# First layers of the paired blocks: three of seven products added in PSUM, attention visits ahead of the fifth product

## The chip, the core and the metric

The kernel runs on one core of one Trainium2 chip. The metric is the device time of one execution in microseconds. Three runs of the kernel before took 792.59, 793.10 and 793.72 us; the median is 793.1 us.

## What is computed

Chunked softmax attention (8 batches, 8 heads, 576 positions of 64 features, in chunks of 64), whose output, laid out as 4608 tokens of 512 features, goes through a two-layer network with a PReLU between:

```python
scores = scale * np.matmul(q_c, k_c.transpose(0, 1, 2, 4, 3))
scores = scores - np.max(scores, axis=-1, keepdims=True)
attn = np.exp(scores)
attn = attn / (np.sum(attn, axis=-1, keepdims=True) + 1e-09)
x = np.matmul(attn, v_c)                  # as tokens: 4608 x 512
h = x @ w_in                              # 512 x 2048
g = np.maximum(h, 0.0) + alpha * np.minimum(h, 0.0)
out = g @ w_out                           # 2048 x 512
```

All of it is float32. A product of two float32 matrices is made of three matmuls on a high and a low part of each operand (high x high, high x low, low x high).

## The kernel before

Tokens come in 36 subtiles of 128 and nine blocks of 512. Attention runs by subtile. A *visit* (`visit`) does the attention of one subtile in two halves: the values (probabilities times v, L361) of the subtile before last, and the scores (L246) of a new one, 32 small matmuls each, into one PSUM tile `ps_a`. Behind them VectorE takes the maximum (L256), ScalarE scales it (L261) and takes eight exponentials, one a head (L263), VectorE normalises (L265 to L267) and transposes (L304), and SP stores and loads the transposed probabilities as `pT` with eight DMAs (L311), for the values of two visits later. ScalarE also copies the values out of `ps_a` into the block's tile xh or xl (L372).

The first three blocks go through both layers plainly, until about 311 us (second layer at L430, its output copied from PSUM at L464). The last six blocks go in three *pairs*. For a pair each layer is a product of 2x2 block matrices made with seven products instead of eight. The first layer of a pair is eight runs of `first_product`, one for each j, of seven products of six matmuls 128x512 (L698), 42 in all. The seven products are summed in four ways; each sum goes through the PReLU into one quarter of g. `prelu` is a negative part on ScalarE (L379) and a multiply-add on VectorE (L382). Four PSUM banks (`ps_o`, called a, c, d and e in `first_product`) take the products; the sums are made in two ways: some products are added to a bank in PSUM, others by VectorE (L720, L727, L728, L738) from a copy that ScalarE makes in SBUF (L719, L726).

The second layer (`second_product`, L841) has 56 steps of six matmuls. Its operands are split into high and low part by a cast on ScalarE (L657) and a subtraction on VectorE (L658), some after an operand subtraction on VectorE (L759); the first few are split while the first layer still runs.

In pairs 0 and 1 each of the eight runs has one visit ahead of it (in the last two of pair 1 with values only); pair 2 has none. Each engine works through its instructions in the order in which the program leaves them. That order comes from a scheduler: instructions under `tc.high_priority` are put forward, and `tc.issue_after` keeps a piece of work behind a named instruction. The visit's softmax is emitted under high priority; TensorE's order is that in which the code is written. Weights of the seven products come from DRAM in units of two products, in the order of the table `ORDERS["wi"]`, through a ring of four buffers that POOL's queue fills (L639).

Of the kernel before, what the change touches and what calls it, by code (L numbers as in the profile page):

```python
# [60 lines left out]
def tile_local_attention_prelu_ffn(  # L61
# [192 lines left out]
    def attn_max(sc3):  # L254
        mx = small.tile([P, H, 1], F32, name="mx", bufs=2)
        return mx, nc.vector.tensor_reduce(mx.rearrange("p (b g) k -> p b (g k)", b=2), sc3, axis=AX.X, op=ALU.max)  # L256

    def attn_softmax(s, sc3, mx, scaled):
        pr = soft.tile([P, H, C], F32, name="pr")
        sm = small.tile([P, H, 1], F32, name="sm", bufs=2)  # L260
        nc.scalar.mul(mx, mx, -SCALE)  # L261
        for g in range(H):
            last = nc.scalar.activation(pr[:, g], sc3[:, g // NP, g % NP], AF.Exp, bias=mx[:, g], scale=SCALE, accum_out=sm[:, g])  # L263
        stages["softmax"] = scaled, last
        nc.vector.tensor_scalar(sm, sm, 1e-9, None, op0=ALU.add)  # L265
        nc.vector.reciprocal(sm, sm)
        nc.vector.tensor_tensor(pr, pr, sm.broadcast_to([P, H, C]), op=ALU.mult)  # L267
        probs[s] = pr

    def early_softmax(s, sc3):  # L270

# [28 lines left out]
    def attn_blocks(s):  # L300

        pr = probs.pop(s)
        tb = stage.tile([P, 2, H, HALF], F32, name="t3", bufs=2)
        nc.vector.transpose(tb.rearrange("p j h t -> p h j t"), pr)  # L304
        pT = load.tile([P, 2, H, HALF], F32, name="pT", bufs=2)
        for c in range(2):
            for i in range(2):
                for j in range(2):
                    src = slice(c * C + i * HALF, c * C + (i + 1) * HALF)
                    dst = slice(c * C + j * HALF, c * C + (j + 1) * HALF)  # L310
                    nc.sync.dma_start(  # L311
                        out=pT[dst, i].rearrange("p h t -> p (h t)"),
                        in_=tb[src, j].rearrange("p h t -> p (h t)"),
                    )
        pdiag[s] = pT
# [68 lines left out]
    def prelu(g, h, f):  # L384
        negative(g, h)
        rectify(g, h, f)
# [95 lines left out]
    phases = [(0, 0, n0), (1, 0, n1), (0, n0, NF), (1, n1, NF)] + [(b, 0, NF) for b in range(2, PLAIN)]  # L482
    x = {0: new_x(), 1: new_x()}

    def visit(old, new):

        ps = ps_a.tile([P, 2, TB], F32, name="ps_a")
        with tc.high_priority(offset=HIGH):
            if old is not None:
                xo = attn_values(old, ps)  # L490
            if new is not None:
                sc3 = attn_scores(new, ps)
                if new + 2 < NSUB:
                    attn_load(new + 2, "q")
                attn_load(new, "v")
            if new is not None:
                attn_softmax(new, sc3, *attn_max(sc3))
            if old is not None:
                attn_x(old, xo)
            if new is not None:  # L500
                attn_blocks(new)

    def visit_two(new):

        tiles = [pool.tile([P, 2, TB], F32, name=name) for pool, name in ((ps_a, "ps_a"), (ps_p, "ps_b"))]
        olds, news = ([s for s in range(n, n + 2) if s < NSUB] for n in (new - 2, new))
        with tc.high_priority(offset=HIGH):
            xs = [attn_values(s, ps) for s, ps in zip(olds, tiles)]
            scores = [attn_scores(s, ps) for s, ps in zip(news, tiles)]
            for s, xo in zip(olds, xs):  # L510
                attn_x(s, xo)
            most = [attn_max(sc3) for sc3 in scores]
        for s in news:
            if s + 2 < NSUB:
                attn_load(s + 2, "q")
            attn_load(s, "v")

        def rest(s, sc3, at):
            attn_softmax(s, sc3, *at)
            attn_blocks(s)  # L520

        return [functools.partial(rest, *args) for args in zip(news, scores, most)]

    def first(which, s, n, queue):

# [38 lines left out]

    ORDERS = {"wi": (5, 7, 1, 6, 3, 4, 2), "wo": (1, 5, 6, 3, 7, 2, 4)}
    units = {side: [dram.tile([P, 2, 2, 2 * P], F32, name=f"{side}_a{n}") for n in range(7 * JF // 2)] for side in ORDERS}

    def unit(side, i, j):  # L570
# [117 lines left out]
    def bank(n):  # L688
        return ps_p.tile([P, TB], F32, name=f"ps_o{n}")
# [10 lines left out]
                    start=first and at == 0, stop=at == n - 1, skip_group_check=not first,  # L700
                ))

    def softmax_behind(read, scored):
        if scored:
            with tc.issue_after(read.ins):
                scored.pop(0)()

    def first_product(ops, g, j, scored):

        def part(ps, i, first):  # L710
            product(ps, weight("wi", i, j), [ops[i, k] for k in range(2)], first)

        c, d, a, e = (bank(n) for n in banks)
        banks[:] = banks[3:] + banks[:3]
        part(c, 5, True)
        part(d, 7, True)
        with tc.high_priority(offset=HIGH):
            t = gp.tile([P, TB], F32, name="gh")
            read = nc.scalar.copy(t, c)  # L719
            nc.vector.tensor_tensor(t, d, t, op=ALU.add)  # L720
        softmax_behind(read, scored)
        part(a, 1, True)
        part(e, 6, True)
        with tc.high_priority(offset=HIGH):
            u = gp.tile([P, TB], F32, name="g")
            read = nc.scalar.copy(u, a)  # L726
            nc.vector.tensor_tensor(u, e, u, op=ALU.add)  # L727
            nc.vector.tensor_tensor(t, t, u, op=ALU.add)  # L728
        softmax_behind(read, scored)
        for n, f in enumerate((j, JF + j)):  # L730
            g[f] = const.tile([P, 2, TB], F32, name=rooms[14 + 2 * j + n])
        with tc.high_priority(offset=HIGH):
            prelu(g[JF + j][:, 1], t, JF + j)
        for ps, i, f, col in ((c, 3, j, 1), (d, 4, JF + j, 0)):
            part(ps, i, False)
            with tc.high_priority(offset=HIGH):
                h = gp.tile([P, TB], F32, name="gl")
                nc.vector.tensor_tensor(h, ps, u, op=ALU.add)  # L738
                prelu(g[f][:, col], h, f)
        part(a, 2, False)  # L740
        with tc.high_priority(offset=HIGH):
            prelu(g[j][:, 0], a, j)

    AHEAD = 2
    EARLIER = 4
# [256 lines left out]
    for pair in range(NPAIR):  # L1002
        b = PLAIN + 2 * pair
        more = pair + 1 < NPAIR
        if more:
            new_raw(b + 2)
        g, scored = {}, []
        for j in range(JF):
            if more:
                visit(new - 2, new if new < NSUB else None)  # L1010
                new += 1
            if j == JF - 1:
                operands = [operand(g, at) for at in range(AHEAD + 1)]
            first_product(ops, g, j, scored)
        if more:
            ops, conversion = convert(b + 2)
        second_product(g, b, operands, conversion, not more)
# [39 lines left out]
```

## Time and profile before

| | |
|---|---|
| median of three runs | 793.1 us (792.59 to 793.72) |
| span of the profiled execution | 791.9 us |
| outside the span, median less span | 1.2 us |
| TensorE busy | 781.9 us (99%) |
| VectorE busy | 654.4 us (83%) |
| ScalarE busy | 448.8 us (57%) |
| first layers of pairs 0, 1, 2 | 85.8, 84.75, 76.1 us |

The span goes from the first to the last instruction that the profiler recorded, and the durations of the rows below are of that one execution. PE is TensorE's matmuls, PEld its weight loads, DVE is VectorE, ACT ScalarE, POOL GpSimd, SP SyncE. In the chain of waits each stretch is put down to the engine on which the end hung. In the timeline a figure in brackets is the idle time ahead of an instruction, and what ended it.

### The profile page before, as it was taken

What the parts mean: (1) busy time and instruction counts of PE and PEld (TensorE: products, weight loads), DVE (VectorE), ACT (ScalarE), POOL (GpSimd) and SP (SyncE); (2) the same over time, 40 slices, a digit from 0 to 9 for tenths busy, and PEclk for the clock granted to TensorE, in tenths of its full rate; (3) what the DMA queues carried; (4) which work ended last, traced back from release to release, by engine and by line L of the source; (5) the groups of instructions that cost most, each with busy time, mean ns of one, the idle gap of its engine ahead of it and who ended that gap; (6) DMA issues with size and microseconds to landing.
All of it is one profiled execution on the core that took longest, in us unless ns stands there. A gap on an engine that the chain in (4) does not pass through costs nothing.

```text
span 791.9 us, 15470 instructions
## 1 busy us (share of the span) xinstructions
PE 781.9 (99%) x5565; PEld 643.2 (81%) x5565; DVE 654.4 (83%) x1153; ACT 448.8 (57%) x1218; POOL 180.9 (23%) x296
## 2 busy tenths in 40 slices
PE   7999999999999999999999999999999999999998
PEld 7788888888888888888888888888888888888886
DVE  6999989997989976877799987777889956679675
ACT  6975555655666565556656546664575444354542
POOL 0053322442324320111111121111211121112110
PEclk9999999999999999999999999999999999999999
DMA  9759495566969675888865778776556766565574
GB/s 345 322 213 363 168 322 197 193 228 184 275 189 285 217 280 172 285 264 272 267 209 196 228 243 281 259 238 193 199 186 220 255 216 190 197 197 188 190 237 158
DMA packets 69467, 184.53 MB, mean 233 GB/s; under 512 B 11008, under 2 KB 18448, under 8 KB 69264
## 3 DMA queue, kind: packets, MB, share of 16 engines
q0 software_dynamic: 34336, 119.56, 45.8%
q1 hardware_dynamic: 34768, 63.60, 23.6%
q8 instruction: 44, 0.72, 0.4%
q10 hardware_dynamic: 288, 0.39, 0.2%
q14 instruction: 31, 0.25, 0.1%
HBM read 135.27 MB, written 42.99 MB: 225 GB/s over the span
## 4 chain that ended last, share of the span: by engine, by line
PE 81%; DVE 6%; ACT 5%; DMA 5%; issue 1%; SPq 1%; POOL 0%; DVEq 0%; ACTq 0%
PE ps_o L698 29%; PE ps_o L841 20%; PE ps_h L394 9%; PE ps_b L841 8%; PE ps_oa L430 5%; PE ps_ob L430 5%; PE ps_a L361 2%; ACT pr L263 1%; DMA pT<-t 1%; PE ps_a L246 1%; DMA wi_a<-raw 1%; DMA raw<-w_out 1%; SPq L311 1%; DMA raw<-w_in 1%; DVE gl L411 1%
## 5 line engine op out<-in xcount | busy, mean ns | idle before, releaser
L394 PE MATMUL ps_h<-xh,wi 128*128 128x512 f32 x384 | 104.5, 394 | 0.2 <-ACT xh L346 0.2
L698 PE MATMUL ps_o<-wi,raw 128*128 128x512 f32 x252 | 99.2, 394 | 0.1
L698 PE MATMUL ps_o<-wo,raw 128*128 128x512 f32 x252 | 98.2, 390 | 0.0
L394 PEld LDWEIGHTS ps_h<-xh,wi 128*128 128x128 f32 x384 | 71.1, 188 | 15.2 <-ACT xh L346 0.4
L263 ACT ACTIVATE pr<-ps_a,mx 128x64 f32<-128x64 f32 x224 | 67.5, 328 | 1.0
L657 ACT CAST gh<-wi 128x512 fp32r<-128x512 f32 x57 | 35.6, 624 | 48.7 <-PE ps_o L841 25.3
L430 PE MATMUL ps_oa<-wo,gh 128*128 128x512 f32 x192 | 59.9, 393 | 0.0
L430 PE MATMUL ps_ob<-wo,gh 128*128 128x512 f32 x192 | 59.1, 389 | 0.0
L698 PEld LDWEIGHTS ps_o<-wi,raw 128*128 128x128 f32 x252 | 47.3, 188 | 10.3 <-ACT wi L464 0.2
L698 PEld LDWEIGHTS ps_o<-wo,raw 128*128 128x128 f32 x252 | 47.3, 188 | 9.6
L394 PE MATMUL ps_h<-xl,wi 128*128 128x512 f32 x192 | 52.0, 390 | 0.0
L698 PE MATMUL ps_o<-wi,wi 128*128 128x512 f32 x126 | 49.6, 394 | 0.0
L698 PE MATMUL ps_o<-wi,wo 128*128 128x512 f32 x126 | 49.6, 394 | 0.0
L263 ACT ACTIVATION_READ_ACCUMULATOR pr<-ps_a,mx 128x1 f32 x224 | 49.3, 220 | 0.0
L698 PE MATMUL ps_o<-wo,wo 128*128 128x512 f32 x126 | 49.1, 390 | 0.0
L698 PE MATMUL ps_o<-wo,wi 128*128 128x512 f32 x126 | 49.1, 390 | 0.0
L408 ACT CAST gh<-g 128x512 fp32r<-128x512 f32 x48 | 30.2, 630 | 31.8 <-DVE g L382 25.8
L720 DVE TENSOR_TENSOR gh<-ps_o,gh 128x512 f32<-128x512 f32 x24 | 16.6, 691 | 38.1 <-ACT gh L719 20.5
L658 DVE TENSOR_TENSOR gl<-wi,gh 128x512 fp32r<-128x512 f32 x54 | 37.2, 690 | 13.1 <-ACT gh L657 12.8
L379 ACT ACTIVATE wo<-gh 128x512 f32<-128x512 f32 x24 | 15.2, 633 | 53.5 <-DVE gh L728 53.5
L639 POOL DMA_DIRECT2D raw<-wi_a x42 | 22.3, 531 | 100.8 <-PE ps_o L698 86.5
L639 POOL DMA_DIRECT2D raw<-wo_a x42 | 22.2, 529 | 94.2 <-PE ps_o L841 52.3
(296 smaller groups left out, 2108.9 us busy)
## 6 DMA issues: line engine op xcount, KB each, us to landing
raw<-wi_a POOLq DMA_DIRECT2D x42, 512.0 KB, 4.5
raw<-wo_a POOLq DMA_DIRECT2D x42, 512.0 KB, 4.4
wi<-wi_a POOLq DMA_DIRECT2D x21, 512.0 KB, 4.5
wo<-wi_a POOLq DMA_DIRECT2D x21, 512.0 KB, 4.7
wi<-wo_a POOLq DMA_DIRECT2D x21, 512.0 KB, 4.3
wo<-wo_a POOLq DMA_DIRECT2D x21, 512.0 KB, 4.5
k_sb<-kT SPq DMA_DIRECT2D x28, 256.0 KB, 4.9
q_sb<-qT SPq DMA_DIRECT2D x28, 256.0 KB, 4.9
```

Of the source, the lines that this page charges most:

```text
L263: last = nc.scalar.activation(pr[:, g], sc3[:, g // NP, g % NP], AF.Exp, bias=mx[:, g], scale=SCALE, accum_out=sm[:, g])
L361: pe(nc.tensor.matmul(ps[par * C:(par + 1) * C, c, hp * C:(hp + 1) * C], lhsT=v_sb[rows, h * C:(h + 1) * C], rhs=p[rows, :, par * NP + hp] ...
L379: nc.scalar.activation(g, h, AF.Relu, scale=-1.0)
L394: pe(nc.tensor.matmul(hps, lhsT=wi[f][:, l, k * P:(k + 1) * P], rhs=xx[:, k], start=(i == 0 and k == 0), stop=(i == 2 and k == NK - 1),))
L408: nc.scalar.copy(gh, g)
L430: pe(nc.tensor.matmul(o, lhsT=a[:, ts], rhs=wo[f][:, l], start=(f == first and i == 0), stop=(f == last and i == 2),))
L639: streamed[0] = nc.gpsimd.dma_start(out=f32(t), in_=units[side][n])
L657: hi = nc.scalar.copy(t_hi, t)
L658: return hi, nc.vector.tensor_tensor(t_lo, t, f32(t_hi), op=ALU.subtract)
L698: pe(nc.tensor.matmul(ps, lhsT=w[:, l, k * P:(k + 1) * P], rhs=xx[:, xl], start=first and at == 0, stop=at == n - 1, skip_group_check=not ...
L720: nc.vector.tensor_tensor(t, d, t, op=ALU.add)
L841: pe(nc.tensor.matmul(ps[m], lhsT=w[:, l, m * P:(m + 1) * P], rhs=xx, start=begins and j == 0 and n == 0, stop=j == JF - 1 and n == 2, ski ...
```

## The change

The order of the seven products in a run goes from 5, 7, 1, 6, 3, 4, 2 to 1, 7, 6, 2, 5, 4, 3. Product 1 goes into bank a. ScalarE copies bank a into bank e, from PSUM to PSUM, and product 6 is added there by TensorE. The sum is copied in the same way into bank c, to which products 5 and then 3 are added; product 2 is added to bank a, product 4 to bank e. Product 7 is copied from bank d into SBUF (v), and VectorE adds it twice: to bank c after product 5 (t) and to bank e after product 4 (u). So a run has two VectorE additions in place of five and three ScalarE copies in place of two, two of them into PSUM; the 42 matmuls stay. The visit of a run now stands after product 2, ahead of the fifth product, in place of ahead of the run. In a visit of a pair the copy of the values now stands ahead of the maximum, and the normalisation, the transpose and its DMAs come behind u. The banks no longer change their parts from run to run.

```diff
@@ -262,10 +262,14 @@
         for g in range(H):
             last = nc.scalar.activation(pr[:, g], sc3[:, g // NP, g % NP], AF.Exp, bias=mx[:, g], scale=SCALE, accum_out=sm[:, g])
         stages["softmax"] = scaled, last
+        return s, pr, sm
+
+    def attn_normalize(s, pr, sm):
         nc.vector.tensor_scalar(sm, sm, 1e-9, None, op0=ALU.add)
         nc.vector.reciprocal(sm, sm)
         nc.vector.tensor_tensor(pr, pr, sm.broadcast_to([P, H, C]), op=ALU.mult)
         probs[s] = pr
+        attn_blocks(s)
 
...
-    def visit(old, new):
+    def visit(old, new, in_pair=False):
 
         ps = ps_a.tile([P, 2, TB], F32, name="ps_a")
         with tc.high_priority(offset=HIGH):
@@ -493,33 +497,16 @@
                 if new + 2 < NSUB:
                     attn_load(new + 2, "q")
                 attn_load(new, "v")
-            if new is not None:
-                attn_softmax(new, sc3, *attn_max(sc3))
-            if old is not None:
+            if in_pair:
                 attn_x(old, xo)
             if new is not None:
-                attn_blocks(new)
...
+                parts = attn_softmax(new, sc3, *attn_max(sc3))
+                if in_pair:
+                    return functools.partial(attn_normalize, *parts)
+            if old is not None and not in_pair:
+                attn_x(old, xo)
+            if new is not None:
+                attn_normalize(*parts)
...
-    ORDERS = {"wi": (5, 7, 1, 6, 3, 4, 2), "wo": (1, 5, 6, 3, 7, 2, 4)}
+    ORDERS = {"wi": (1, 7, 6, 2, 5, 4, 3), "wo": (1, 5, 6, 3, 7, 2, 4)}
...
-    def softmax_behind(read, scored):
-        if scored:
-            with tc.issue_after(read.ins):
-                scored.pop(0)()
-
-    def first_product(ops, g, j, scored):
+    def first_product(ops, g, j, between):
 
         def part(ps, i, first):
             product(ps, weight("wi", i, j), [ops[i, k] for k in range(2)], first)
 
-        c, d, a, e = (bank(n) for n in banks)
-        banks[:] = banks[3:] + banks[:3]
-        part(c, 5, True)
+        a, d, e, c = (bank(n) for n in banks)
+        for n, f in enumerate((j, JF + j)):
+            g[f] = const.tile([P, 2, TB], F32, name=rooms[14 + 2 * j + n])
+        part(a, 1, True)
+        with tc.high_priority(offset=HIGH):
+            nc.scalar.copy(e, a)
         part(d, 7, True)
         with tc.high_priority(offset=HIGH):
-            t = gp.tile([P, TB], F32, name="gh")
-            read = nc.scalar.copy(t, c)
-            nc.vector.tensor_tensor(t, d, t, op=ALU.add)
-        softmax_behind(read, scored)
-        part(a, 1, True)
-        part(e, 6, True)
+            v = gp.tile([P, TB], F32, name="g")
+            nc.scalar.copy(v, d)
+        part(e, 6, False)
         with tc.high_priority(offset=HIGH):
-            u = gp.tile([P, TB], F32, name="g")
-            read = nc.scalar.copy(u, a)
-            nc.vector.tensor_tensor(u, e, u, op=ALU.add)
-            nc.vector.tensor_tensor(t, t, u, op=ALU.add)
-        softmax_behind(read, scored)
-        for n, f in enumerate((j, JF + j)):
-            g[f] = const.tile([P, 2, TB], F32, name=rooms[14 + 2 * j + n])
-        with tc.high_priority(offset=HIGH):
-            prelu(g[JF + j][:, 1], t, JF + j)
-        for ps, i, f, col in ((c, 3, j, 1), (d, 4, JF + j, 0)):
-            part(ps, i, False)
-            with tc.high_priority(offset=HIGH):
-                h = gp.tile([P, TB], F32, name="gl")
-                nc.vector.tensor_tensor(h, ps, u, op=ALU.add)
-                prelu(g[f][:, col], h, f)
+            nc.scalar.copy(c, e)
         part(a, 2, False)
         with tc.high_priority(offset=HIGH):
             prelu(g[j][:, 0], a, j)
+        normalize = between()
+        part(c, 5, False)
+        with tc.high_priority(offset=HIGH):
+            t = gp.tile([P, TB], F32, name="gh")
+            nc.vector.tensor_tensor(t, c, v, op=ALU.add)
+            prelu(g[JF + j][:, 1], t, JF + j)
+        part(e, 4, False)
+        with tc.high_priority(offset=HIGH):
+            u = gp.tile([P, TB], F32, name="gl")
+            summed = nc.vector.tensor_tensor(u, e, v, op=ALU.add)
+            if normalize:
+                with tc.issue_after(summed.ins):
+                    normalize()
+            prelu(g[JF + j][:, 0], u, JF + j)
+        part(c, 3, False)
+        with tc.high_priority(offset=HIGH):
+            prelu(g[j][:, 1], c, j)
 
...
-        g, scored = {}, []
+        g = {}
         for j in range(JF):
+            between = lambda: None
             if more:
-                visit(new - 2, new if new < NSUB else None)
+                between = functools.partial(visit, new - 2, new if new < NSUB else None, True)
                 new += 1
             if j == JF - 1:
                 operands = [operand(g, at) for at in range(AHEAD + 1)]
-            first_product(ops, g, j, scored)
+            first_product(ops, g, j, between)
         if more:
             ops, conversion = convert(b + 2)
         second_product(g, b, operands, conversion, not more)
```

Three places show how the engines' orders change. The first is TensorE, at the end of the plain phase (`ps_ob` is its last output bank) and the start of pair 0. Here before:

```order
L430 MATMUL ps_ob<-wo_1527,gl 128x512
L361 MATMUL ps_a<-pT,v_sb 64x64 x16
L246 MATMUL ps_a<-k_sb,q_sb 64x64 x16
L698 MATMUL ps_o_4038<-wi_3807,raw 128x512
L698 MATMUL ps_o_4038<-wo_3808,raw 128x512
```

And now, where `ps_o_3971` is bank a, `ps_o_3972` d, `ps_o_3973` e and `ps_o_3974` c:

```order
L434 MATMUL ps_ob<-wo_1527,gl 128x512
L685 MATMUL ps_o_3971<-wi_3434,raw 128x512
L685 MATMUL ps_o_3971<-wo_3435,raw 128x512
...
L685 MATMUL ps_o_3972<-wi_3798,raw 128x512
...
L685 MATMUL ps_o_3973<-wi_3847,raw 128x512
...
L685 MATMUL ps_o_3971<-wi_3589,raw 128x512
...
L365 MATMUL ps_a<-pT,v_sb 64x64 x16
L246 MATMUL ps_a<-k_sb,q_sb 64x64 x16
L685 MATMUL ps_o_3974<-wi_3807,wi_3924 128x512
```

The first visit has moved from between the two phases to behind four products of the first run.

The second is VectorE in the first run of pair 0, from the end of the plain phase's work. Before (`mx` is the maximum, `gh`, `g` and `gl` the sums, `ta` and `tb` the high and low part of a split operand):

```order
L256 TENSOR_REDUCE mx<-ps_a 128x8
L720 TENSOR_TENSOR gh<-ps_o_4039,gh 128x512
L265 TENSOR_SCALAR sm<-sm 128x8
L266 RECIPROCAL sm<-sm 128x8
L267 TENSOR_TENSOR pr<-pr,sm 128x512
L304 STREAM_TRANSPOSE t_4027<-pr 128x8x2x32
L727 TENSOR_TENSOR g<-ps_o_4041,g 128x512
L728 TENSOR_TENSOR gh<-gh,g 128x512
L738 TENSOR_TENSOR gl<-ps_o_4038,g 128x512
```

And now (L715 is t, L720 is u):

```order
L386 SCALAR_TENSOR_TENSOR wi_3975<-wi_3975,rise,ps_o_3971 128x512
L645 TENSOR_TENSOR tb<-wi_3975,ta 128x512
L256 TENSOR_REDUCE mx<-ps_a 128x8
L715 TENSOR_TENSOR gh<-ps_o_3974,g 128x512
L720 TENSOR_TENSOR gl<-ps_o_3973,g 128x512
L386 SCALAR_TENSOR_TENSOR wo_3976<-wo_3976,rise,gh 128x512
L268 TENSOR_SCALAR sm<-sm 128x8
L269 RECIPROCAL sm<-sm 128x8
L270 TENSOR_TENSOR pr<-pr,sm 128x512
L386 SCALAR_TENSOR_TENSOR wo_3976<-wo_3976,rise,gl 128x512
L386 SCALAR_TENSOR_TENSOR wi_3975<-wi_3975,rise,ps_o_3974 128x512
L308 STREAM_TRANSPOSE t_4085<-pr 128x8x2x32
```

Three additions are gone; product 2's prelu and the split of its result now stand ahead of the maximum, and the maximum stands directly ahead of t. On ScalarE the cast for that split (L644) stands between the negative part of product 2 and the copy of the values, and the maximum waits for the copy. The second run has a split (into `more`) at the same place.

The third is VectorE in the sixth run of pair 0 and the visit in it. Before, between the prelu that ends the fifth run and the run's first addition:

```order
L382 SCALAR_TENSOR_TENSOR wi_4781<-wi_4781,rise,ps_o_4744 128x512
L256 TENSOR_REDUCE mx<-ps_a 128x8
L658 TENSOR_TENSOR more<-wi_4781,more 128x512
L759 TENSOR_TENSOR wi_4357<-wi_4357 128x512
L720 TENSOR_TENSOR gh<-ps_o_4883,gh 128x512
L265 TENSOR_SCALAR sm<-sm 128x8
```

And now, from product 2's prelu:

```order
L386 SCALAR_TENSOR_TENSOR wi_4664<-wi_4664,rise,ps_o_4660 128x512
L645 TENSOR_TENSOR more<-wi_4664,more 128x512
L744 TENSOR_TENSOR wi_4249<-wi_4249 128x512
L256 TENSOR_REDUCE mx<-ps_a 128x8
L715 TENSOR_TENSOR gh<-ps_o_4663,g 128x512
L720 TENSOR_TENSOR gl<-ps_o_4662,g 128x512
```

The split and an operand subtraction (L744) have moved from behind the maximum to ahead of it and of t. In pair 1 the first, second and sixth run have the same order.

## Rows read from the trace of the kernel before

**Rows 1.** The page: span; busy us (share) xinstructions by engine; granted TensorE clock in tenths.

```profile
span 791.9 us, 15470 instructions
...
PE 781.9 (99%) x5565; PEld 643.2 (81%) x5565; DVE 654.4 (83%) x1153; ACT 448.8 (57%) x1218; POOL 180.9 (23%) x296
...
PEclk9999999999999999999999999999999999999999
```

**Rows 2.** Busy time by stretch: from:to, length, engines (instructions), clock, DMA share, GB/s.

```profile
311.90:397.70 85.80, 85.73 (x785) 70.01 (x786) 66.05 (x113) 53.21 (x196) 14.27 (x27) 1.00 0.85 273
...
475.00:559.75 84.75, 84.75 (x725) 69.06 (x722) 63.10 (x105) 49.72 (x163) 14.38 (x28) 1.00 0.74 240
...
635.90:712.00 76.10, 76.10 (x338) 63.05 (x337) 50.17 (x75) 31.29 (x54) 14.81 (x28) 1.00 0.62 200
```

**Rows 3.** The chain that ended last, in order of time: start, length, what.

```profile
310.84 1.08 ACT wi L464 x2
...
321.82 0.62 PE ps_a L361 x32
322.44 0.47 PE ps_a L246 x32
322.91 9.75 PE ps_o L698 x42
...
635.91 76.16 PE ps_o L698 x336
```

**Rows 4.** Waits of TensorE from 104 us on: total us, times, longest.

```profile
PE ps_a L361 <- DMA pT<-t: 0.3, 1, 0.3
```

**Rows 5.** Timeline, TensorE where the pairs begin: start, length, engine, line, operation.

```profile
310.73 0.69 PE L361 MATMUL ps_a<-pT,v_sb 64*64 64x64 f32 x32
...
311.25 0.65 PE L246 MATMUL ps_a<-k_sb,q_sb 64*64 64x64 f32 x32
...
311.96 0.51 PE L698 MATMUL ps_o<-wi,raw 128*128 128x512 f32 x1
...
312.31 0.40 PE L698 MATMUL ps_o<-wo,raw 128*128 128x512 f32 x1
```

**Rows 6.** Timeline of pair 0: SP's pT loads, one split, two VectorE additions in a row.

```profile
317.86 4.97 SPq L311 DMA_DIRECT2D pT<-t  x8
...
333.99 0.74 DVE L382 SCALAR_TENSOR_TENSOR wi<-wi,rise,ps_o 128x512 f32<-128x512 f32 x1
...
334.77 0.62 ACT L657 CAST more<-wi 128x512 fp32r<-128x512 f32 x1 [1.47 <-DVE wi L382]
...
335.43 0.69 DVE L658 TENSOR_TENSOR more<-wi,more 128x512 fp32r<-128x512 f32 x1
...
341.70 1.28 DVE L738 TENSOR_TENSOR gl<-ps_o,g 128x512 f32<-128x512 f32 x2
```

**Rows 7.** Groups by line and shape, 311.9 to 397.7: busy us, mean ns.

```profile
L256 DVE TENSOR_REDUCE mx<-ps_a 128x8 f32<-128x512 f32 x8 | 5.5, 687 | 4.8 <-PE ps_a L246 4.8
...
L379 ACT ACTIVATE wo<-gh 128x512 f32<-128x512 f32 x8 | 5.1, 633 | 17.9 <-DVE gh L728 17.9
...
L379 ACT ACTIVATE wi<-ps_o 128x512 f32<-128x512 f32 x7 | 4.1, 584 | 0.0
...
L372 ACT COPY xh<-ps_a 128x512 f32<-128x512 f32 x4 | 2.5, 636 | 0.0
```

**Rows 8.** Timeline of pair 2: two products' first matmuls, and readers of the bank before.

```profile
637.11 0.39 PE L698 MATMUL ps_o<-wi,raw 128*128 128x512 f32 x1
...
637.36 0.59 ACT L719 COPY gh<-ps_o 128x512 f32<-128x512 f32 x1 [0.83 <-PE ps_o L698]
...
638.47 0.39 PE L698 MATMUL ps_o<-wi,raw 128*128 128x512 f32 x1
...
638.74 0.69 DVE L720 TENSOR_TENSOR gh<-ps_o,gh 128x512 f32<-128x512 f32 x1 [3.42 <-PE ps_o L698]
```

**Rows 9.** Waits of TensorE up to 104 us, the longest.

```profile
PE ps_ob L322 <- ACT wo L289: 1.4, 1, 1.4
```

More of the change, by code (lines that the diff above doesn't have):

```diff
@@ L495, in visit @@
                 attn_load(new, "v")
-            if new is not None:
-                attn_softmax(new, sc3, *attn_max(sc3))
-            if old is not None:
+            if in_pair:
                 attn_x(old, xo)
             if new is not None:
-                attn_blocks(new)
-    def visit_two(new):
-        tiles = [pool.tile([P, 2, TB], F32, name=name) for pool, name in ((ps_a, "ps_a"), (ps_p, "ps_b"))]
-        olds, news = ([s for s in range(n, n + 2) if s < NSUB] for n in (new - 2, new))
-        with tc.high_priority(offset=HIGH):
[L508 to L522, printed above, removed]
+                parts = attn_softmax(new, sc3, *attn_max(sc3))
[5 more added lines that the diff above has]
+                attn_normalize(*parts)
     def first(which, s, n, queue):
@@ L701, in product @@
                 ))
-    def softmax_behind(read, scored):
-        if scored:
-            with tc.issue_after(read.ins):
-                scored.pop(0)()
-    def first_product(ops, g, j, scored):
+    def first_product(ops, g, j, between):
         def part(ps, i, first):
             product(ps, weight("wi", i, j), [ops[i, k] for k in range(2)], first)
-        c, d, a, e = (bank(n) for n in banks)
-        banks[:] = banks[3:] + banks[:3]
-        part(c, 5, True)
+        a, d, e, c = (bank(n) for n in banks)
[4 more added lines that the diff above has]
+            nc.scalar.copy(e, a)
         part(d, 7, True)
         with tc.high_priority(offset=HIGH):
-            t = gp.tile([P, TB], F32, name="gh")
-            read = nc.scalar.copy(t, c)
-            nc.vector.tensor_tensor(t, d, t, op=ALU.add)
-        softmax_behind(read, scored)
-        part(a, 1, True)
-        part(e, 6, True)
-        with tc.high_priority(offset=HIGH):
-            u = gp.tile([P, TB], F32, name="g")
-            read = nc.scalar.copy(u, a)
-            nc.vector.tensor_tensor(u, e, u, op=ALU.add)
-            nc.vector.tensor_tensor(t, t, u, op=ALU.add)
-        softmax_behind(read, scored)
-        for n, f in enumerate((j, JF + j)):
-            g[f] = const.tile([P, 2, TB], F32, name=rooms[14 + 2 * j + n])
-        with tc.high_priority(offset=HIGH):
-            prelu(g[JF + j][:, 1], t, JF + j)
-        for ps, i, f, col in ((c, 3, j, 1), (d, 4, JF + j, 0)):
-            part(ps, i, False)
-            with tc.high_priority(offset=HIGH):
-                h = gp.tile([P, TB], F32, name="gl")
-                nc.vector.tensor_tensor(h, ps, u, op=ALU.add)
-                prelu(g[f][:, col], h, f)
+            v = gp.tile([P, TB], F32, name="g")
+            nc.scalar.copy(v, d)
+        part(e, 6, False)
+        with tc.high_priority(offset=HIGH):
+            nc.scalar.copy(c, e)
         part(a, 2, False)
```

## The prediction

> **What bounds the kernel now.** I read the page first, then busy time by stage, then the chain of waits, then what TensorE waited for, and last the timeline of the places that the change touches. The page [rows 1] gives TensorE 99% of the span at a granted clock of full speed throughout (2.4 GHz, the higher of its two levels); VectorE has 83%, ScalarE 57%. The table by stage [rows 2] says the same of the part that is changed: in the first layers of pairs 0, 1 and 2 (311.9 to 397.7, 475.0 to 559.8, 635.9 to 712.0) TensorE is busy for all but 0.07 us, while VectorE has 66.1, 63.1 and 50.2 us of work. The reader should see that VectorE's load is no limit in those stages: whatever is taken from it is taken from slack.
>
> The chain [rows 3] runs on TensorE alone there, with one exception: at 310.84 ScalarE's copies out of the plain phase's last bank, 1.08 us, after which the pairs begin at 311.96. The list of waits confirms it: from 104 us on TensorE as a whole has one wait of 0.3 us [rows 4]. So the stage is 24 runs of 42 matmuls. Without visits eight runs take 76.16 us [rows 3], 9.52 each and 1.36 a product. From one visit's end to the next one's start 9.75 pass and the visit adds 0.62 + 0.47 [rows 3]: 10.84 a run, so a visit costs 10.84 - 9.52 = **1.32 us** of TensorE time.
>
> **What no longer matters.** Three of five VectorE additions go in each of 24 runs. At 0.69 us [rows 8] that is 72 x 0.69 = 50 us of VectorE, and 24 more ScalarE copies at 0.6 cost it 14 us. The matmuls stay the same in number and size. No row shows TensorE waiting for those additions, so their removal is worth 0, with 0.2 us as the most it can give (the 0.3 us wait, whose releaser is another, aside). What counts is the waits that the new order makes.
>
> **Step 1: the first visit leaves its shelter.** Before, the first visit of pair 0 stands between the plain phase's last matmul and the pairs' first. Its matmuls run from 310.73 to 311.90 [rows 5], while ScalarE empties ps_ob until 311.91, for which the pairs' first matmul waits anyway (311.96). It costs nothing there. In the changed order the matmuls of product 1 follow directly, wait for the same copies, and the visit comes after product 2. All eight visits of pair 0 are then paid: **+1.32 us**. The matmul after such a wait loses 0.05 to its release and 0.12 more (the second issues 0.35 after it, where the pitch is 0.23 [rows 5]); 0.17 is what I add to every release below.
>
> **Step 2: one run in a clock of its own**, 0 being the first issue of product 1. Products begin at 0, 1.36, 2.72 and 4.08; the visit lies at 5.44 to 6.76; then come the fifth product at 6.76, the fourth at 8.12, the third at 9.48; the run ends at 10.84. A reader of a finished bank starts 0.25 (ScalarE) or 0.27 (VectorE) after the next product's first issue (637.11 to 637.36 and 638.47 to 638.74 [rows 8]).
>
> - The copy of bank a into e: no row shows ScalarE writing PSUM. The nearest, ScalarE reading PSUM and writing SBUF, take 0.58 to 0.64 [rows 7]; I take the 0.59 of the copy in rows 8. It runs from 1.61 to 2.20, wanted at 2.72 - 0.17 = 2.55. It fits below 0.94 us. The copy c from e (4.33 to 4.92) is wanted only at 6.6. Both cost 0, and cheaper copies would change nothing; the upper bound is a rival below.
> - Product 2's negative part: 5.69 to 6.27. The copy of the attention result (0.64 [rows 7]) now stands ahead of the maximum on ScalarE, and the maximum waits for it, since both read one tile. The visit's last matmul ends 1.26 after it begins, at 6.70; the copy takes 6.75 to 7.38, the maximum (0.69 [rows 7]) 7.42 to 8.11.
> - t = c + v stands behind the maximum on VectorE and also needs the fifth product: 8.39 to 9.08. The third product goes into the same bank, so it is wanted at 9.48 - 0.17 = 9.31. **A slack of 0.23 us**, where before no product waited for a VectorE read within one product of its bank's last matmul. Plain runs: 0.
>
> **Step 3: the runs in which an operand is split early.** The scheduler puts the first splits of the second layer's operands into runs 1, 2 and 6 of pairs 0 and 1, between product 2's prelu and the maximum, as the order of VectorE shows. In the trace the cast follows the prelu's end (333.99 + 0.74) by 0.04 and takes 0.62; its subtraction follows 0.04 after [rows 6]. Independent VectorE operations follow each other at 0.60 (two in 1.28 [rows 6]).
>
> - Runs 1 and 2: negative until 6.27, VectorE's half 6.32 to 7.06, cast 7.10 to 7.72, and only then the attention copy, until 8.33 (a pitch of 0.60 behind the cast). Split 7.76, maximum 8.36, t 8.96 to 9.65: 0.34 after 9.31.
> - Run 6 has an operand subtraction (priced like an addition, 0.69) between split and maximum as well: split 7.76, subtraction 8.36, maximum 8.96, t 9.56 to 10.25: 0.94 after 9.31.
>
> In two pairs: 2 x (0.34 + 0.34 + 0.94) = **+3.24 us**. Pair 2 has no visits: t runs 7.07 to 7.76 and is wanted at 7.99, so it costs 0.
>
> **Step 4: tails.** After a late maximum the eight exponentials move too, and the next run's copy into e stands behind them on ScalarE. In a plain run it waits for its matmuls alone. In run 6 exponentials, three negative parts and the copy end at about 14.3 of that run's clock against 14.33 wanted (13.39 and the 0.94 already lost). I book **+0.2**, between 0 and 1.
>
> The normalisation moves behind u, and with it the transpose and SP's eight loads of pT: the transpose ends at about 14.5 of the run and the values are wanted two visits later at 27.1. A lag of 12.6 holds SP's issue, which took 4.97 us for all eight [rows 6]. 0, and at worst the 0.3 us that this wait has once now [rows 4]. The weight stream's order is that of the units, still one per two products: 0.
>
> **Sum.** 1.32 + 3.24 + 0.20 = 4.76 us. The profiled span of 791.9 becomes 796.7; the median of the runs is 1.2 above the span, so about **797.8 us**, 0.6% more. From no change a measurement of this kernel can tell about 0.2%, which is 1.6 us.
>
> **Rivals.**
> 1. *Only step 1 remains* (not slower by what can be told). t is late by 0.34 at most in four runs and 0.94 in two; if the casts are taken sooner than I book, or VectorE takes the maximum and t closer behind each other than 0.60, runs 1 and 2 fall away; run 6 needs 0.94 less over five links. It decides where t ends before 9.31 in all of them. Then 791.9 + 1.3 + 1.2 = 794.4. For it: my pitches are those of engines that ran without cross waits. Against it: the order is fixed, each link is a row, and run 6 is 0.94 late.
> 2. *Copies into PSUM are slow.* At twice the row, 1.2 us, the copy into e ends at 2.81, 0.26 late in each of 24 runs: 6.2 more, 804.0. Against it: reading PSUM costs no more than reading SBUF (0.584 against 0.633 [rows 7]), so that bank access is not dear. The Trainium skill, ScalarE: Activation LUTs, "Step-by-step: what each stage is for", says that ScalarE reaches PSUM sooner than SBUF; by that the copies stay under the row's figure and the sum stands. No row shows it yet.
> 3. *The clock falls.* The changed runs stop TensorE for some tenths of a us about six times. In the trace it stopped 1.4 us for a ScalarE copy in the early phase [rows 9] and the granted clock stayed 1.00 [rows 1]. One run at the lower level (1.2 GHz) costs 9.52 more: 807. The Trainium skill, TensorE: Matmul & The Clock Gate, "A second HAM failure mode: psum-queue depth-cycling", tells of a kernel in which short idle times between groups of matmuls, made by cycling through banks, kept throttling the clock. The rows here speak against that at stops of this length.
> 4. *Faster.* VectorE's 50 us would have to hide a wait. TensorE has none in these stages beyond 0.07 us [rows 2]; only if all of steps 1 to 4 came to nothing and the plain phase, whose order is nearly the same, gained by chance. At most 791.9 - 0.3 + 1.2 = 792.8 and so still no difference that can be told.
>
> **How the numbers follow.** The forecast has 66%; its own range is 796 to 799.5 (runs 1 and 2 without stall: 3.4 in all; tails of 1 and another 0.6 in run 6's followers: 6.2). Rival 1 has 20%, slow copies 5%, the clock 2%, other stalls that I don't see 2%, something faster 5%. Slower by over 0.2%: 66 + 5 + 2 + 2 = 75%; within: 20%; faster: 5%. The range takes in rival 1 and part of the slow copies: 794.2 to 800.8.
>
> **What would show it.** The chain after should leave TensorE in runs 1, 2 and 6 of pairs 0 and 1, where the waits name the VectorE addition t as releaser of the third product, about 0.3, 0.3 and 0.9 us; runs 3 to 5 and pair 2 should be as long as now (10.84 and 9.52). Between the plain phase's last matmul and the pairs' first there should be no visit, and TensorE should be idle there for about 1.1 us. The copies into PSUM should take about 0.6 us; over 0.94 and product 6 waits in every run. Wrong would be: a first layer of pair 0 no longer than 85.8 + 1.4 (t is in time), a wait in every visited run (a slack of 0.23 was too much), a wait for pT, or a granted clock under 1.00.

## The result, and the profile after

The changed kernel takes 798.46 us (median of four runs, 798.09 to 798.52); the kernel before took 792.85 us beside it. The ratio is 1.0068, with a 95% interval of 1.0054 to 1.0082: slower, by 5.6 us. The profiled execution has a span of 796.6 us, 4.7 more than before. The two differences are not the same because the profiled execution before was a long one: the time is 1.7 to 1.8 us above the span in all four runs here and in 29 of 37 later runs of the kernel before, whose median span is 791.3. By that a span of 791.9 belongs to a time of about 793.7, the longest of the first three. This is the page after the change (as in [rows 1]):

```profile
span 796.6 us, 15334 instructions
...
PE 784.6 (98%) x5565; PEld 641.9 (81%) x5565; DVE 610.9 (77%) x1081; ACT 463.5 (58%) x1242; POOL 180.9 (23%) x296
...
PEclk9999999999999999999999999999999999999999
```

VectorE has lost 72 instructions and 43.5 us of work, ScalarE has gained 24 and 14.7 us, TensorE has the same 5565 matmuls at the same clock, and the end comes later. The stretches of the first layers of pairs 0 and 2, as in [rows 2]:

```profile
311.60:400.68 89.08, 88.40 (x849) 70.38 (x850) 52.04 (x87) 57.90 (x202) 14.28 (x27) 1.00 0.77 253
...
640.60:716.80 76.20, 76.20 (x338) 63.12 (x337) 35.11 (x52) 36.23 (x61) 14.81 (x28) 1.00 0.62 201
```

Pair 2, which has no visits, is as long as it was; pair 0 is 3.3 us longer. TensorE's waits from 104 us on, which were one of 0.3 us [rows 4], are now:

```profile
PE ps_o L685 <- DVE gh L715: 1.2, 2, 0.6
PE ps_o L685 <- ACT wi L468: 1.2, 1, 1.2
```

and those of its weight loads, which show the short ones too (a weight load runs ahead of its matmul, so its wait is longer than what TensorE loses):

```profile
PEld ps_o L685 <- DVE gh L715: 3.8, 6, 1.0
...
PEld ps_o L685 <- ACT ps_o L700: 1.5, 7, 0.3
```

L715 is t: it holds the third product (the one numbered 3, which stands last in a run) up six times. L468 are the plain phase's last copies, under which the first visit used to stand. L700 is the copy into bank e: seven small waits. The chain shows where they lie (start, length, what), to be read against [rows 3]:

```profile
310.52 1.08 ACT wi L468 x2
...
311.65 5.78 PE ps_o L685 x24
317.42 0.62 PE ps_a L365 x32
...
318.51 2.95 PE ps_o L685 x12
321.47 7.20 PE ps_o L685 x30
...
341.01 9.75 PE ps_o L685 x42
...
362.69 9.76 PE ps_o L685 x42
372.47 0.61 ACT wi L383
...
373.11 0.76 DVE wi L386
373.89 0.63 ACT more L644
...
374.54 0.69 DVE more L645
375.23 0.60 DVE wi L744
375.83 0.60 DVE mx L256
376.43 0.61 DVE gh L715
...
377.09 7.19 PE ps_o L685 x30
384.28 0.62 PE ps_a L365 x32
...
640.65 76.16 PE ps_o L685 x336
```

A run without a stall still has 9.75 between two visits (341.01). In run 1 the fifth and fourth products and the rest take 2.95 + 7.20 = 10.15, 0.40 more. In run 6 the chain leaves TensorE: from product 2's negative part at 372.47 over its other half, the cast, the split, the operand subtraction and the maximum to t, and back to TensorE at 377.09. From the visit's start at 372.45 to the next one's at 384.28 are 11.83 where a plain run has 10.84.

Stage by stage, by the chains of the two traces: the plain phase is 0.31 us shorter (the pairs begin at 311.65), pair 0's first layers take 89.03 in place of 85.74 (+3.29), pair 1's with their first visit 87.59 in place of 85.79 (+1.80), the rest is 0.08 shorter: 4.70 in all. I do not put the 0.31 down to the change: in the ten profiled executions of this study the pairs began between 311.2 and 315.3 us, in kernels whose plain phases are nearly the same. The experiments below are therefore compared by stage.

### The profile page after: what moved, and what is told of

It is laid out like the page before. It is cut to its first block, busy times and chain, and to the rows that moved or that the text cites. A ratio compares the mean times of both kernels' runs of the same rounds, so it can differ in the third digit from the quotient of the medians.

```text
span 796.6 us, 15334 instructions
## 1 busy us (share of the span) xinstructions
PE 784.6 (98%) x5565; PEld 641.9 (81%) x5565; DVE 610.9 (77%) x1081; ACT 463.5 (58%) x1242; POOL 180.9 (23%) x296
## 4 chain that ended last, share of the span: by engine, by line
PE 96%; ACT 2%; DVE 1%; issue 0%; ACTq 0%
PE ps_o L685 29%; PE ps_o L826 20%; PE ps_h L398 17%; PE ps_oa L434 8%; PE ps_ob L434 8%; PE ps_b L826 8%; PE ps_a L365 2%; PE ps_a L246 2%; ACT wo L293 1%; PE ps_h L878 1%; ACT wi L293 1%; ACT xh L350 0%; PE ps_a L344 0%; ACT wo L333 0%; PE ps_ob L326 0%; DVE wi L386 0%
## 5 line engine op out<-in xcount | busy, mean ns | idle before, releaser
L386 DVE SCALAR_TENSOR_TENSOR wi<-wi,rise,ps_o 128x512 f32<-128x512 f32 x48 | 35.7, 745 | 92.1 <-ACT wi L383 92.0
L644 ACT CAST gh<-wi 128x512 fp32r<-128x512 f32 x57 | 35.6, 624 | 48.5 <-PE ps_o L826 25.5
L398 PEld LDWEIGHTS ps_h<-xl,wi 128*128 128x128 f32 x192 | 36.0, 188 | 7.8
```

The source lines that it names most:

```text
L386: nc.vector.scalar_tensor_tensor(g, in0=g, scalar=rise[:, f:f + 1], in1=h, op0=ALU.mult, op1=ALU.add)
L398: pe(nc.tensor.matmul(hps, lhsT=wi[f][:, l, k * P:(k + 1) * P], rhs=xx[:, k], start=(i == 0 and k == 0), stop=(i == 2 and k == NK - 1),))
L644: hi = nc.scalar.copy(t_hi, t)
```

## The experiments

All times by stage are from one matmul's issue to another's, read from the traces: where the pairs begin, the first layers of pair 0, from there to the end of pair 1's first layers, the first layers of pair 2, the span.

| kernel | begin | pair 0 | to the end of pair 1's | pair 2 | span | ratio of times to before (95%) |
|---|---|---|---|---|---|---|
| before | 311.96 | 85.57 | 162.04 | 76.16 | 791.9 | |
| changed | 311.65 | 88.87 | 163.82 | 76.16 | 796.6 | 1.0068 (1.0054 to 1.0082) |
| 1 late splits | 311.19 | 87.86 | 162.80 | 76.16 | 794.1 | 1.0037 (1.0025 to 1.0048) |
| 2 copy back | 311.36 | 90.15 | 165.19 | 76.16 | 799.0 | 1.0083 (1.0064 to 1.0102) |
| 3 early matmuls | 313.38 | 87.13 | 163.77 | 76.16 | 796.5 | 1.0043 (1.0026 to 1.0060) |
| 4 both of 1 and 3 | 315.27 | 86.32 | 162.87 | 76.16 | 796.7 | 1.0023 (1.0011 to 1.0035) |
| 5 and the cast held | 311.48 | 85.73 | 161.98 | 76.16 | 791.5 | 1.0007 (0.9998 to 1.0016) |
| 6 visits ahead | 311.28 | 91.80 | 165.95 | 76.16 | 801.3 | 1.0140 (1.0124 to 1.0157) |
| 7 double copy | 312.29 | 93.32 | 166.70 | 77.83 | 806.3 | 1.0180 (1.0166 to 1.0194) |
| 8 place alone | 311.40 | 92.61 | 168.94 | 76.16 | 805.2 | 1.0179 (1.0165 to 1.0192) |

### 1. Splits held behind u

```diff
             summed = nc.vector.tensor_tensor(u, e, v, op=ALU.add)
+            sums[j] = summed.ins
...
-        behind[:] = behind[1:] + [split(t, hi, lo)]
+        with tc.issue_after(sums[at]) if at in (0, 1, 5) else nullcontext():
+            behind[:] = behind[1:] + [split(t, hi, lo)]
```

> The changed kernel, but the splits of the second layer's operands in runs 1, 2 and 6 are held back until u of the same run. Theory (t is late because a cast on ScalarE and a split, in run 6 an operand subtraction too, stand ahead of the maximum and so of t): the third product waits in no run; 2 x 1.50 us of waits for t go, and about 0.7 of the later waits for the copy into e that follow from them. Span 796.6 - 3.7 = 792.9, about 794.7 us. Rival A (the copy of the values ahead of the maximum is what makes t late, whatever the split does): the waits stay, span 796.6. Rival B (the copies into PSUM cost it): span 796.6.

2.0 us of the 3.7 went: 1.0 in each pair. The waits for t did not vanish: what they cost, the slow matmul behind each of them included, fell from 0.30, 0.30 and 0.90 to 0.18 in each of these runs. The timeline of run 6 tells why (start, length, engine, operation, [idle before and its releaser]):

```profile
373.14 0.62 ACT L644 CAST more<-wi 128x512 fp32r<-128x512 f32 x1 [0.82 <-DVE wi L386]
...
373.67 0.58 ACT L376 COPY xl<-ps_a 128x512 f32<-128x512 f32 x1
...
374.28 0.69 DVE L256 TENSOR_REDUCE mx<-ps_a 128x8 f32<-128x512 f32 x1 [1.17 <-ACT xl L376]
...
374.89 0.68 DVE L716 TENSOR_TENSOR gh<-ps_o,g 128x512 f32<-128x512 f32 x1
...
375.63 0.50 PE L686 MATMUL ps_o<-wi,raw 128*128 128x512 f32 x1
```

The edit moved VectorE's half of the split only. The cast on ScalarE still stands ahead of the copy of the values, the copy ahead of the maximum, the maximum ahead of t. So the edit took out one half of what the theory names: 0.12 (in run 6 0.72) is the split ahead of the maximum. The 0.18 that stays is either the cast ahead of the copy, the other half, or the copy's place alone (rival A). Experiment 5 decides that.

### 2. The copy of the values put back behind the exponentials

```diff
-            if in_pair:
-                attn_x(old, xo)
             if new is not None:
                 parts = attn_softmax(new, sc3, *attn_max(sc3))
-                if in_pair:
-                    return functools.partial(attn_normalize, *parts)
-            if old is not None and not in_pair:
+            if old is not None:
                 attn_x(old, xo)
+            if new is not None and in_pair:
+                return functools.partial(attn_normalize, *parts)
```

> The changed kernel, but in a visit of a pair the values are copied out behind the exponentials, as before the change; the splits stay ahead of the maximum on VectorE. Theory (the split's place is what counts): the maximum still follows the split, so t is as late as in the changed kernel, 0.30, 0.30 and 0.90 us in runs 1, 2 and 6 of two pairs; the copy now stands between the exponentials and the next run's copy into e, which comes about 0.5 us later after each of these runs, up to 2.5 us more in all: span 797 to 799. Rival A (the copy ahead of the maximum makes t late): the waits for t go, span 796.6 - 3.0 to 3.7 = 793 to 793.6. Rival B: no change, 796.6.

The waits for t stayed at 0.30, 0.30 and 0.90, and the copy into e came late in the six runs that follow, at a cost of 0.55 to 0.57 in each:

```profile
PE ps_o L683 <- ACT ps_o L698: 1.6, 6, 0.3
PE ps_o L683 <- DVE gh L713: 1.2, 2, 0.6
```

So with the split on VectorE ahead of the maximum it makes no difference to t where the copy stands, and moving it ahead was right: behind the exponentials it pushes the next run's copy into e.

### 3. The first visit's matmuls under the plain phase's last copies

```diff
             if more:
-                between = functools.partial(visit, new - 2, new if new < NSUB else None, True)
+                made = visit_matmuls(new - 2, new) if pair == 0 and j == 0 else None
+                between = functools.partial(visit, new - 2, new if new < NSUB else None, True, made)
```

(`visit_matmuls` is the part of `visit` that issues matmuls and loads; the rest takes `made` where it is given, and its maximum and exponentials are then issued after the copy into c.)

> The changed kernel, but the matmuls of pair 0's first visit stand ahead of the pairs' first product again, under the wait for the plain phase's last copies; its maximum and exponentials are held back behind the run's copy into c. Theory: 1.32 us of TensorE time in pair 0 go under that wait, and in run 1 of pair 0 the maximum comes early, so that its t is in time as well (0.30 and 0.1 behind it). Span 796.6 - 1.7 = 794.9, about 796.7 us. Rival C (the first visit was not hidden before, the pairs merely begin later): span unchanged but for the 0.4 of run 1, 796.2.

Pair 0 is 1.74 shorter, as worked out, and pair 1 unchanged. The profiled span does not show it, since in that execution the plain phase was 1.7 longer, 1.0 of it in a wait that the kernel before does not have:

```profile
PE ps_oa L434 <- ACT more L468: 1.0, 1, 1.0
```

It lies in the output of an earlier block, in code that the edit leaves alone. The profiled execution of experiment 4 had it at 2.0 us, and its other runs are faster (median 795.06 us, 3.4 below the profiled one). Why it comes in some executions stays open.

### 4. Both

> Both of the above in one: first visit's matmuls ahead of the pairs, splits of runs 1, 2 and 6 behind u. Theory: nothing of the loss is left, span 796.6 - 1.32 - 3.77 = 791.5, 0.4 under the kernel before (the plain phase is 0.3 shorter), about 792.6 to 793.3 us, no difference from before that can be told although VectorE has 72 additions less. Rival D (VectorE's load was worth something that the losses covered): a span clearly under 791, down to 789. Rival B (copies into PSUM cost it): more than 793.

Pair 0 is 2.55 shorter than in the changed kernel and pair 1's stretch 0.95: the sum of 1 and 3, less run 1 of pair 0, in which both edits remove the same wait. What is left is the 0.18 that experiment 1 found and the late copies into e behind it. By stage the span would be 793.1, which is rival B's figure as well; experiment 5 tells the two apart, since it leaves the copies into PSUM in place. Ratio to before 1.0023: still slower.

### 5. The cast held behind the copy of the values as well

```diff
+            if in_pair:
+                taken[0] = attn_x(old, xo)
...
+            sums[j] = taken[0] and taken[0].ins, summed.ins
...
+        with ExitStack() as held:
+            if at in (0, 1, 5) and sums[at][0]:
+                for one in sums[at]:
+                    held.enter_context(tc.issue_after(one))
+            behind[:] = behind[1:] + [split(t, hi, lo)]
```

> As the run with both edits, and in runs 1, 2 and 6 ScalarE's cast for the split is held back too, behind the copy of the values (the run before had moved VectorE's half of the split alone, and 0.18 us of the wait for t stayed in each of these runs, and 0.1 of the wait for the copy into e behind each). Theory: t is late by the cast ahead of the copy (0.18) and by the split ahead of the maximum (0.12, in run 6 0.72). With both out of the way the third product waits in none of these runs and the copy into e comes in time after them; pair 0's first layers take 1.98 us less than in the changed kernel's chain for the waits and 1.6 less for the visit, pair 1's 1.8 less. Counted by stage, with the plain phase of the changed kernel: 791.6 of span, 792.7 to 793.4 us, as before the change. Rival A' (0.18 stays because of the copy ahead of the maximum alone, whatever the cast does): 0.18 + 0.13 stays in each of the five runs, 1.5 us more.

All of it went. From one visit to the next it is 10.84 again, in pair 1 with values only 10.38 as before, but for one wait that costs 0.17 in run 8 of pair 0. Against the changed kernel pair 0 is 3.14 shorter and pair 1's stretch 1.84 (the expectation's 1.98 and 1.6 for pair 0 count run 1's wait twice). Page and chain:

```profile
span 791.5 us, 15335 instructions
...
PE 782.1 (99%) x5565; PEld 642.8 (81%) x5565; DVE 609.9 (77%) x1081; ACT 464.6 (59%) x1242; POOL 181.4 (23%) x296
```

```profile
310.35 1.08 ACT wi L467 x2
...
311.48 15.28 PE ps_o L692 x66
...
382.05 9.92 PE ps_o L692 x42
```

The 1.08 us of copies hide a visit again, so that 66 matmuls follow before the next one. Rival A' falls: it was the cast. And this kernel settles what the 72 additions are worth: it has 44.5 us less of VectorE work than the kernel before, no other new wait of TensorE, and takes the same time, 793.46 against 793.15 us, ratio 1.0007 (0.9998 to 1.0016), so that a gain over 0.2 us is ruled out.

### 6. The sums in PSUM, the visits where they were

```diff
-            first_product(ops, g, j, between)
+            normalize = between()
+            first_product(ops, g, j, lambda: normalize)
```

> The changed kernel with the three products added in PSUM as they are, but each visit ahead of its run, where it stood before the change. Theory: t is no longer behind the maximum and the first visit is under the plain phase's last copies, but now the eight exponentials, 0.29 each, lie on ScalarE between the copy into e and the copy into c, and there is no visit on TensorE between product 2 and the fifth: the copy into c ends about 0.6 us late in each of 14 runs, 8.4 us. Span about 800, pair 2 unchanged at 76.16. Rival B' (adding in PSUM is free wherever the visit stands): 791.6. Rival E (the fifth product's t is late here too): over 803.

The mechanism and its size were right: the fifth product waits 14 times.

```profile
PE ps_o L685 <- ACT ps_o L707: 4.9, 14, 0.8
```

It costs 0.61 in a usual run (0.48 at the wait and 0.13 at the next matmul), about 1.0 in runs 7 and 8 of pair 0, and three times the next visit's start is 0.34 to 0.38 late as well: 801.3 where I had 800. The two runs of pair 1 whose visit has values only, and so no exponentials, do not wait. ScalarE in the third run of pair 0, whose first matmul is at 334.12, shows it:

```profile
335.82 0.57 ACT L700 COPY ps_o<-ps_o 128x512 f32<-128x512 f32 x1 [0.97 <-PE ps_o L685]
...
336.67 0.31 ACT L263 ACTIVATE pr<-ps_a,mx 128x64 f32<-128x64 f32 x1
...
339.48 0.65 ACT L707 COPY ps_o<-ps_o 128x512 f32<-128x512 f32 x1
```

2.8 us of exponentials and another copy lie between the copy into e and the copy into c, and TensorE would reach the fifth product 5.58 after the run's first matmul, at 339.70. Behind product 2, the place that the change gives the visit, the exponentials come after both copies.

### 7. The copy into e made twice

```diff
             nc.scalar.copy(e, a)
+            nc.scalar.copy(e, a)
```

> The changed kernel with the copy from bank a into e made twice in each run. My estimate was that the copy is wanted 2.55 us after product 1's first matmul and ends at 2.20 if it takes 0.59; the trace shows 0.57, so a second one ends at 2.7 to 2.8. Theory: product 6 waits 0.13 to 0.2 in each of the 17 runs in which the copy came in time, pair 2's eight among them (76.16 becomes 77.2 to 77.8), and 0.5 more in each of the seven in which it came late: 5.7 to 7.4 us, span 802.3 to 804. Rival F (there is more slack than the 0.35 worked out): pair 2 stays at 76.16, span 796.6 to 800.

Pair 2 became 1.67 longer, 0.27 in its first run and 0.20 in each of the other seven, and a plain run of pairs 0 and 1 by 0.20. Two rows of ScalarE in pair 2 and the matmul that waits for them:

```profile
659.82 0.57 ACT L700 COPY ps_o<-ps_o 128x512 f32<-128x512 f32 x1 [0.76 <-PE ps_o L685]
...
660.42 0.57 ACT L701 COPY ps_o<-ps_o 128x512 f32<-128x512 f32 x1
...
661.04 0.50 PE L685 MATMUL ps_o<-wi,raw 128*128 128x512 f32 x1
```

The second ends at 660.99, where 660.81 would have been in time (0.17 ahead of 660.98, six issues of 0.226 after 659.62 as before): 0.18, and 0.20 was lost. So the deadline holds: the copy has some 0.4 us to spare and no more. The total is 2 us over what I gave: 0.6 in the plain phase (with a wait of 1.1 for pT there), and 1.8 in run 8 of pair 0 where the others lost 0.2 to 0.6: there the two copies did not stay together, and the copy of bank d and a cast stood between them on ScalarE.

### 8. The visit's new place alone, in the kernel before

```diff
-            if more:
-                visit(new - 2, new if new < NSUB else None)
+            between = lambda: None
+            if more:
+                between = functools.partial(visit, new - 2, new if new < NSUB else None)
                 new += 1
...
         part(e, 6, True)
+        between()
```

> The kernel before with one part of the change alone: each visit stands behind the fourth of the seven products (order 5, 7, 1, 6, 3, 4, 2 as it was), sums by VectorE as they were. Theory: the first visit comes out from under the plain phase's last copies, 1.32 us, and nothing else is lost, since there no product goes into a bank whose sum VectorE has read one product earlier: pair 0's first layers 1.3 us longer by the chain, pair 1 and 2 as before, span 793.2. Rival G (the visit's place alone makes TensorE wait, whatever the sums): pair 1's first layers longer as well, by 1.5 to 1.8 us, span 796.

Both were wrong by far: it costs 7.0 in pair 0 and 6.9 in pair 1's stretch, 14 us by the medians. The first visit's 1.32 is among them; nearly all the rest is

```profile
PE ps_o L698 <- DVE wi L382: 7.9, 12, 0.7
...
PE ps_o L842 <- DVE tb L658: 1.0, 1, 1.0
```

The second line is one step of the second layer that waits for a split. In twelve runs the fourth in order, product 6, costs 0.95 more (0.82 at the wait, 0.13 behind it), waiting for the last prelu of the run before, whose bank it takes. In the third run of pair 0 the last matmul ahead of it starts at 338.04, and then:

```profile
339.09 0.50 PE L698 MATMUL ps_o<-wi,raw 128*128 128x512 f32 x1 [0.66 <-DVE wi L382]
```

With the visit in the middle of the run its eight exponentials and the normalisation stand ahead of the prelu of the last sums on ScalarE and VectorE, and with rotating banks that one is needed early. I had looked for a sum that is read too late and not for a bank that comes free too late. So the visit's new place is not free by itself, and the parts of the change need each other. That it is the fixed banks, needed late in a run, and the normalisation behind u that make room for the visit there is argued from the order; no run takes them away one by one.

## Why the prediction was right

The forecast was 797.8 us at a span of 796.7; measured were 798.46 and 796.6. By its steps:

- *The first visit, +1.32.* Right. TensorE stands idle at 310.52 to 311.65, with no visit in it, and putting the visit's matmuls back there (3) took 1.74 from pair 0: 1.32, the 0.30 of run 1's t, which then has its maximum early, and 0.1 behind it.
- *Plain runs, 0.* Right: 9.75 between visits in runs 4 and 5 of either pair, 76.16 in pair 2; in run 4 of pair 0 t ends 9.01 after the run's first matmul, where I had 9.08 and 9.31 as the latest.
- *Copies into PSUM, 0.59.* They take 0.57:

```profile
L700 ACT COPY ps_o<-ps_o 128x512 f32<-128x512 f32 x8 | 4.9, 607 | 2.0 <-PE ps_o L685 1.8
...
L704 ACT COPY g<-ps_o 128x512 f32<-128x512 f32 x8 | 4.7, 587 | 4.3 <-PE ps_o L685 4.3
...
L707 ACT COPY ps_o<-ps_o 128x512 f32<-128x512 f32 x8 | 4.6, 570 | 6.0 <-PE ps_o L685 6.0
```

  (607 is a mean with those that follow another operation closely, 0.65.) The rival of slow copies falls, and 7 shows the deadline that it would have had to miss.
- *t late in runs 1, 2 and 6, +3.24.* Right in place, mechanism and nearly in size: 0.30, 0.30 and 0.90 in each pair, 3.00. In run 6 t ends at 377.04, 10.20 after the run's first matmul at 366.84, where I had 10.25:

```profile
376.36 0.68 DVE L715 TENSOR_TENSOR gh<-ps_o,g 128x512 f32<-128x512 f32 x1
...
377.09 0.50 PE L685 MATMUL ps_o<-wi,raw 128*128 128x512 f32 x1 [0.61 <-DVE gh L715]
377.42 0.40 PE L685 MATMUL ps_o<-wo,raw 128*128 128x512 f32 x1
```

  The working named both links, the cast ahead of the copy and the split ahead of the maximum; 1 and 5 removed one after the other and took the wait away in two parts. The expectation of 1 named both too, but its edit moved the split alone, and that this would take the whole wait away was wrong.
- *Tails, +0.2.* The term that was too small: 0.77, 0.1 each in runs 2, 3 and 7 of both pairs and 0.16 in run 8 of pair 0. I had looked at run 6's follower alone and found 0.03 to spare. Run 2 of pair 0, first matmul at 322.96:

```profile
324.46 0.64 ACT L383 ACTIVATE wi<-ps_o 128x512 f32<-128x512 f32 x1
...
324.94 0.65 ACT L700 COPY ps_o<-ps_o 128x512 f32<-128x512 f32 x1
...
325.70 0.43 PE L685 MATMUL ps_o<-wi,raw 128*128 128x512 f32 x1
```

  The copy into e ends 2.63 after the run's first matmul, 0.08 later than wanted: operations behind one another on ScalarE take 0.65 each in place of 0.57, and exponentials that begin about 1 us later than in a plain run (9.45 after the first matmul of run 1, 8.34 in run 4) leave no room. The 0.16 in run 8 has another cause, and stays when all else is gone (5). In run 7 of pair 0, first matmul at 378.58, the maximum comes in time, but all eight exponentials stand behind t's negative part on ScalarE and begin at 9.68:

```profile
387.72 0.63 ACT L383 ACTIVATE wo<-gh 128x512 f32<-128x512 f32 x1 [0.73 <-DVE gh L715]
388.26 0.30 ACT L263 ACTIVATE pr<-ps_a,mx 128x64 f32<-128x64 f32 x1
```

  In a plain run five of them come ahead of it. Why the scheduler ordered this run otherwise is not shown.
- *VectorE's 72 additions, 0.* Right, shown by 5. (They were 43.5 us of work, 0.60 each, where I had 50.)
- *Outside the span, 1.2.* Too small: 1.7 to 1.8 in each run of the changed kernel. I had set the median of three runs beside the span of one long execution. This is why the time is 0.7 above the forecast while the span agrees to 0.1.
- *Rival 1* (t in time after all) would have left +1.3; *the clock* stayed at 1.00 through stops of 0.2 to 1.2 us, as [rows 9] let expect.

That the sum came out at 4.70 beside 4.76 is partly luck: 1.32 + 3.00 + 0.77 = 5.09, and the plain phase and the rest gave back 0.39, which I take for the spread of executions. By the medians the change costs 5.6 us, with 4.3 to 6.5 as the interval; 5.09 lies in it, and so does the forecast's 4.76.

## What to carry to other kernels

Where TensorE is busy for 99% of a stage, taking work from another engine has little to give (in experiment 5, 44.5 us less of VectorE work gave nothing); such a change is judged by the waits that it makes, and a bank that is read between two products that go into it puts a deadline of one product (1.36 us here) on the reader. On engines that work in order, the price of a new order is read by laying one period out in a clock of its own and asking, for each operation with a deadline, what stands in front of it; the optional work that a scheduler fills in (here early splits) belongs in that row too. Before moving a piece of work, look whether it stands under a wait that stays: what it hid there has to be paid elsewhere.

## What the runs showed of the hardware

- ScalarE copies 128x512 float32 from PSUM to PSUM in 0.570 us and from PSUM to SBUF in 0.587 (rows above). The Trainium skill, ScalarE: Activation LUTs, "Step-by-step: what each stage is for", calls PSUM the quicker destination; the trace agrees, by 3%.
- TensorE adds to a bank that ScalarE filled at the pace at which it adds to one of its own: product 6 takes 1.36 us like the others, 76.16 us for pair 2's 336 matmuls before and after.
- A matmul that waits loses about 0.13 us beyond the wait: the next one follows 0.33 to 0.35 after it, where the pitch is 0.23 (377.09 and 377.42).
